# Windowed attention and a two-layer network in one kernel on Trainium2: in the list schedule of the later groups, the margin ahead of transposes and value products is doubled

## The chip, the cores and the metric

The kernel runs on one core of one Trainium2 chip. The metric is the device time of one execution in microseconds (us). The kernel before took 711.27 us, the median of three runs (710.24, 711.27 and 713.42).

## The reference

The inputs are q, k and v of 4 batches x 8 heads x 768 positions x 64, and two weights of 512 x 2048 and 2048 x 512, all float32. Each position attends to the first 8 positions and to the 96 behind and including itself, with a bias that falls with the distance; the heads are joined and go through a network with an ELU between its two layers.

```python
scores = scale * q @ k.T - slope[h] * dist          # slope[h] = 2 ** -(h + 1)
scores = where(is_global | is_local, scores, -1e9)  # is_global: column < 8; is_local: 0 <= row - column < 96
a = softmax(scores); attn = a @ v                   # per batch and head
x = attn, heads side by side: (4 * 768) x 512
h = x @ w_in
out = where(h > 0, h, exp(min(h, 0)) - 1) @ w_out   # (4 * 768) x 512
```

## The kernel before

**The work.** The 3072 positions are cut into 12 groups of 256 (two tiles of 128). For each group the kernel does attention for four pairs of heads (`pair`, which calls `head` once for each head of a pair) and then the network (`moe`) in 16 slices of 128 hidden columns. Products are split into a high and a low part, so a slice takes twelve matmuls 128x256 into a tile h (L606) and six matmuls 128x512 into the accumulators o (L628). Between them ACT and DVE make the ELU (L612 to L614), ACT rounds it to gh (L287 `copy`) and POOL takes the remainder gl (L295 `minus`).

**Attention of the later groups.** The first four groups take another path (`heads32`). From the fifth group on `head` does, for one head and each of its two tiles of positions: two matmuls for the scores s (L561); on DVE the table, the bias and the row's maximum (L478); on ACT the exponential and its sum (L480); once for both tiles the inverse on DVE (L487, L488); on DVE the scaling (L468); on PE one or two transposes of the probabilities pr into a tile t (L575); on ACT a rounding copy of t into pt (L287), on DVE the remainder into the other half of pt (L295); and on PE one or two value products of pt with vd into a tile pv (L587). When a head's two tiles are there, `pair` moves pv to x (ACT L287 once, DVE L459 twice), and after both heads of a pair x goes to xh (ACT) and xl (POOL), which the group's network reads. Each pair loads its q and v (rqv, L405) and its keys (rk, L406) by a DMA on SP's queue and splits them beforehand: qd (ACT L432), ks (ACT L287, then DVE L295 on 64 partitions), ql (DVE L437) and vd (POOL L289 and L295).

**Buffers.** The PSUM tiles have few slots: s two, h two, and t, pv, o0 and o1 one each. In the other memory pr has three slots, pt two, and rqv and rk one each.

**What sets the order.** Nothing is put in order by hand. `Plan.add` records each step with its cost, its engine, its reads and writes and a due time; `Plan.order` is a list scheduler that takes, over all five engines, the step that can start first and, among those that can start now, the one due first, and so fixes the order of each engine's queue. On the chip each engine then works through its queue in that order and waits at its head for what is not ready. The planner's durations are not the chip's. For a step on PE the planner lets it start only some time after its operands' planned end: a fixed 90 ns (`SEM`) and the step's `slack`. For the slot of a tile that the step is the first to write, only 0.3 of the slack is added:

```python
                    for of, t in op.ready.items():                                                          # L133
                        t = t + self.SEM + op.slack if of != e else t - self.LAT["PE"] if e == "PE" else t  # L135
                        at = max(at, t)                                                                     # L136
...
                        at = max(at, f + self.SEM + 0.3 * op.slack)                                         # L152
```

The steps with a slack are those of `head` on PE: the scores (L563), the transposes (L577) and the value products (L590). All have `SLACK` = 600 ns. The network's steps have none. While a margin runs, the planner gives PE other work that can start, mostly the network's matmuls of the group before.

## Time and profile before

| | |
|---|---|
| runs of the kernel before | 711.27 us median of 3 (710.24 to 713.42) |
| the profiled execution | 711.18 us, of which the span from first to last instruction 709.4 us |
| mean granted TensorE clock | 0.998 |
| busy: PE / PE weight loads / DVE / ACT / POOL | 98% / 87% / 73% / 71% / 35% of the span |
| transposes of the later groups (L575) | 240 matmuls, first at 212.3 us, last at 645.0 us |
| value products of the later groups (L587) | 240 matmuls, first at 215.9 us, last at 647.3 us |
| last matmul starts | 702.59 us |

In a row of the profile, PE is the matmul, PEld the loading of its stationary operand, DVE, ACT and POOL are the vector, scalar and general engines and SP is the one whose queue issues most DMAs. `out<-in` names the tiles that an instruction writes and reads. A timeline row gives the start (us), the time that it covers (us), engine, line, operation, tiles, how many instructions it stands for, and in brackets how long the engine sat idle just before and what ended that. Matmuls overlap, and their ends are modelled, so the distance from start to start tells more than the durations.

### The profile page before, as it was taken

To read this page: it belongs to the slowest core of one execution; us is meant where nothing else is said; L and a number is where in the kernel's file an instruction comes from. 1 tells how busy PE (TensorE), PEld (TensorE's weight loads), DVE (VectorE), ACT (ScalarE), POOL (GpSimd) and SP (SyncE) were. 2 spreads that over 40 slices of the span, in tenths; PEclk is the share of its full clock that TensorE was granted. 3 is DMA by queue.
4 is the path that set the end of the run, shared out by engine and by line. 5 is a ranking of instruction groups with operands and counts; after the bars stand their busy time and mean duration, and the time that the engine had idled before them with its cause. 6 is when DMAs were issued, how large, how long until landed. Compare 5 with 4: busy or idle time off the path is not lost.

```text
span 709.4 us, 13834 instructions
## 1 busy us (share of the span) xinstructions
PE 693.8 (98%) x4701; PEld 615.0 (87%) x4701; DVE 517.3 (73%) x1571; ACT 504.0 (71%) x1463; POOL 246.5 (35%) x274
## 2 busy tenths in 40 slices
PE   9989999999999999999999999999999999999996
PEld 6768888889898989999989999999989989999895
DVE  6999999996658958856766875884783884884322
ACT  6989887774657758867767876876776785875442
POOL 2430543440023443433453452542443354332000
PEclk9999999999999999999999999999999999999999
DMA  8443960000233212312312222230331321210000
GB/s 322 176 127 132 419 274 24 1 24 1 76 105 94 82 54 83 107 54 84 107 54 83 80 81 64 73 106 31 107 83 40 107 71 51 84 54 1 31 1 34
DMA packets 22254, 63.49 MB, mean 89 GB/s; under 512 B 2592, under 2 KB 4896, under 8 KB 22176
## 3 DMA queue, kind: packets, MB, share of 16 engines
q1 hardware_dynamic: 21888, 62.40, 26.3%
q8 instruction: 39, 0.64, 0.4%
q14 instruction: 39, 0.32, 0.1%
q10 hardware_dynamic: 288, 0.13, 0.1%
HBM read 56.23 MB, written 6.29 MB: 88 GB/s over the span
## 4 chain that ended last, share of the span: by engine, by line
PE 71%; DVE 16%; DMA 6%; ACT 4%; issue 2%; SPq 1%; DVEq 0%; ACTq 0%
PE h L606 29%; PE o L628 29%; PE pv L587 4%; PE s L561 4%; DMA bits<-in_w_out_dram 4%; PE t L575 3%; DVE g L372 2%; DVE g L374 2%; DVE e L614 2%; DVE w L295 1%; DVE gl L295 1%; DVE pr L478 1%; DVE ks L295 1%; DMA rqv<-in_qkv_dram 1%; DVE pr L468 1%
## 5 line engine op out<-in xcount | busy, mean ns | idle before, releaser
L606 PEld LDWEIGHTS h<-xh,w 128*128 128x128 f32 x1536 | 228.2, 189 | 26.5 <-issue 1.0
L606 PE MATMUL h<-xh,w 128*128 128x256 f32 x1536 | 245.7, 283 | 0.3 <-DVE e L614 0.3
L628 PE MATMUL o<-w,gh 128*128 128x512 f32 x768 | 243.7, 399 | 1.3 <-DVE w L295 0.4
L295 POOL TENSOR_TENSOR gl<-e,gh 128x256 fp32r<-128x256 f32 x133 | 101.8, 765 | 263.5 <-ACT gh L287 253.8
L628 PEld LDWEIGHTS o<-w,gh 128*128 128x128 f32 x768 | 126.2, 189 | 15.2 <-ACT gh L287 2.8
L614 DVE SCALAR_TENSOR_TENSOR e<-e,h 128x256 f32<-128x256 f32 x192 | 80.0, 417 | 73.0 <-ACT e L613 64.5
L628 PE MATMUL o<-w,gl 128*128 128x512 f32 x384 | 133.0, 400 | 0.0
L612 ACT ACTIVATE e<-h 128x256 f32<-128x256 f32 x192 | 73.3, 382 | 74.6 <-PE h L606 67.4
L606 PE MATMUL h<-xl,w 128*128 128x256 f32 x768 | 123.6, 283 | 0.0
L287 ACT CAST gh<-e 128x256 fp32r<-128x256 f32 x192 | 77.4, 403 | 54.1 <-DVE e L614 53.1
L606 PEld LDWEIGHTS h<-xl,w 128*128 128x128 f32 x768 | 104.2, 189 | 0.3 <-issue 0.2
L478 DVE CUSTOM_DVE_ANT_0 pr<-s,tab 128x256 f32<-128x256 f32 (+1 forms) x192 | 73.4, 395 | 42.5 <-PE s L561 37.5
L480 ACT ACTIVATE pr<-pr,nmax 128x256 f32<-128x256 f32 (+1 forms) x192 | 93.6, 488 | 13.4 <-DVE nmax L478 12.7
L613 ACT ACTIVATE e<-e 128x256 f32<-128x256 f32 x192 | 80.1, 418 | 4.2
L369 POOL TENSOR_SCALAR g<-g 128x512 f32<-128x512 f32 x25 | 54.3, 2180 | 69.9 <-ACT g L367 65.2
L459 DVE TENSOR_TENSOR x<-pv,x 64x256 f32<-64x256 f32 x128 | 53.7, 419 | 21.3 <-ACT x L287 18.7
L628 PEld LDWEIGHTS o<-w,gl 128*128 128x128 f32 x384 | 63.7, 189 | 2.2
L468 DVE TENSOR_SCALAR pr<-pr,st 128x256 f32<-128x256 f32 (+1 forms) x159 | 62.2, 421 | 1.2
L287 ACT CAST pt<-t 128x256 fp32r<-128x256 f32 (+1 forms) x128 | 45.5, 355 | 20.9 <-PE t L575 20.3
L295 DVE TENSOR_TENSOR pt<-t,pt 128x256 fp32r<-128x256 f32 (+1 forms) x128 | 51.5, 402 | 11.6 <-ACT pt L287 10.8
L575 PE MATMUL t<-ident,pr 128*128 128x128 f32 x240 | 47.4, 273 | 2.8 <-DVE pt L295 2.5
L587 PE MATMUL pv<-pt,vd 128*128 128x256 f32 x240 | 49.5, 289 | 0.1
(92 smaller groups left out, 880.7 us busy)
## 6 DMA issues: line engine op xcount, KB each, us to landing
rqv<-in_qkv_dram SPq DMA_DIRECT2D x32, 512.0 KB, 3.5
rk<-in_qkv_dram SPq DMA_DIRECT2D x32, 400.0 KB, 3.2
bits<-in_w_in_dram SPq DMA_DIRECT2D x16, 512.0 KB, 9.0
bits<-in_w_out_dram SPq DMA_DIRECT2D x16, 512.0 KB, 9.7
rqv<-in_qkv_dram SPq DMA_DIRECT2D x16, 384.0 KB, 3.6
out_dram<-ob SPq DMA_DIRECT2D x23, 256.0 KB, 2.0
rk<-in_qkv_dram SPq DMA_DIRECT2D x16, 200.0 KB, 4.8
out_dram<-ob ACTq DMA_DIRECT2D x1, 128.0 KB, 2.6
```

The costliest lines, as they stand in the source:

```text
L287: self.nc.scalar.copy(out, x)
L295: self.on(e).tensor_tensor(out, x, y, ALU.subtract)
L468: self.nc.vector.tensor_scalar(out, x, sc, None, ALU.mult)
L478: p.add((("DVE", 158 + 1.042 * n, False),), lambda e: nc.vector.tensor_tensor_reduce(pr.t[:, lo:], s.t[:, m, lo:], tab, -(2.0 ** -(h + 1)) ...
L480: p.add(act(n, extra=200), lambda e: nc.scalar.activation(pr.t[:, lo:], pr.t[:, lo:], AF.Exp, bias=nm, scale=-1.0, accum_out=st.t[:, 0, i: ...
L575: nc.tensor.transpose(tp.t[:, a], pr.t[:, a * P:(a + 1) * P], self.ident.t)
L587: nc.tensor.matmul(pv.t[:, i].rearrange("p s w -> p (s w)"), vd.t[:, 2 * i + a, j].rearrange("p s d -> p (s d)"), pt.t[:, a].rearrange("p ...
L606: nc.tensor.matmul(h.t, w1.t[:, s, cc * P:(cc + 1) * P], x.t[:, cc], start=n == 0 and cc == 0, stop=n == 2 and cc == self.NCC - 1)
L612: p.add(act(W, True), lambda e: nc.scalar.activation(ex.t, h.t, AF.Relu, scale=-1.0), [h], [ex], d - 8000)
L613: p.add(act(W), lambda e: nc.scalar.activation(ex.t, ex.t, AF.Exp, scale=-1.0), [ex], [ex], d - 8000)
L614: p.add(dve(W), lambda e: nc.vector.scalar_tensor_tensor(ex.t, ex.t, -1.0, h.t, ALU.add, ALU.max), [h, ex], [ex], d - 8000)
L628: nc.tensor.matmul(acc[i].t, g.t[:, i * P:(i + 1) * P], w2.t[:, s], start=fc == f0 and n == 0 and s == HI, stop=fc == f1 - 1 and n == 1)
```

## The change

The transposes and the value products get a margin of their own, `LATER` = 1200 ns; the scores keep 600 ns. Nothing is added or removed, and no duration, due time or slot changes. Since the planner's times move, so does the order of the steps on every engine from the fifth group's attention on.

```diff
@@ head
-            p.add((("PE", 75.0 * (2 - a0), False),), transposes, [pr], [tp], d - 2500, slack=slack)
+            p.add((("PE", 75.0 * (2 - a0), False),), transposes, [pr], [tp], d - 2500, slack=self.LATER)
...
-            p.add((("PE", 122.0 * (2 - a0), False),), values, [vd, pt], [pv], d, slack=slack)
+            p.add((("PE", 122.0 * (2 - a0), False),), values, [vd, pt], [pv], d, slack=self.LATER)
@@ class Kernel
-    SLACK = 600.0
+
+    SLACK, LATER = 600.0, 1200.0
```

The lines below `SLACK` move down by one (L786 becomes L787). Up to the first transpose of the fifth group PE's queue is the same row for row. Three places of the queues are shown, before and after the change. In the names the first number is that of the tile, the same in both kernels, and the second differs between them.

PE, in the seventh group's attention, around the two transposes t_1108 and t_1110 of one head; h_988 and h_992 are tiles of the network, pv and pt those of value products. Before:

```order
L575 MATMUL t_1108_5041<-ident_67,pr_1105_4956 128x128
L606 MATMUL h_988_5016<-xl_12_3944,w0_401_1735 128x256 x4
L628 MATMUL o_950_4535<-w1_392_1719,gl_983_4966 128x512
L628 MATMUL o_951_4578<-w1_392_1719,gl_983_4966 128x512
L628 MATMUL o_950_4535<-w1_398_1790,gh_986_5032 128x512 x2
L606 MATMUL h_992_5066<-xh_11_3928,w0_407_1863 128x256 x4
L575 MATMUL t_1110_5074<-ident_67,pr_1107_4964 128x128 x2
L587 MATMUL pv_1102_5078<-pt_1109_5047,vd_1099_4834 128x256
L628 MATMUL o_951_4578<-w1_398_1790,gh_986_5032 128x512 x2
```

And now, from the first four matmuls of h_992 on:

```order
L606 MATMUL h_992_5051<-xh_11_3956,w0_407_1863 128x256 x4
L628 MATMUL o_951_4573<-w1_398_1790,gh_986_5008 128x512 x2
L575 MATMUL t_1108_5064<-ident_67,pr_1105_4947 128x128
L606 MATMUL h_992_5051<-xh_11_3956,w0_407_1863 128x256 x4
L606 MATMUL h_992_5051<-xl_12_3962,w0_407_1863 128x256 x4
L587 MATMUL pv_1085_5029<-pt_1094_5036,vd_1072_4658 128x256 x2
L628 MATMUL o_950_4535<-w1_398_1790,gl_987_5019 128x512
L575 MATMUL t_1110_5091<-ident_67,pr_1107_4994 128x128 x2
```

t_1110 stood right behind the first four matmuls of h_992 and now stands behind two o, eight h and one o more of the network; t_1108 has moved by more than that, so fewer matmuls lie between the two. The value product of t_1108's pt, which stood right behind t_1110, now comes eight rows below it.

DVE, in the same place: the scaling of pr_1107 (L468), which t_1110 reads, the remainder of the next keys ks_1193 (L295, 64x800), and the remainder pt_1109 (L295), the last reader of t_1108. Before:

```order
L468 TENSOR_SCALAR pr_1107_4964<-pr_1107_4964,st_1103_4968 128x256
L295 TENSOR_TENSOR ks_1193_5022<-rk_1191_4902,ks_1193_5022 64x800
L459 TENSOR_TENSOR x_1074_4986<-pv_1085_5024,x_1074_4986 64x256
L478 ISA pr_1117_5055,nmax_71<-s_1116_5004,tab1_69 128x256
L478 ISA nmax_71 128x1
L295 TENSOR_TENSOR pt_1109_5047<-t_1108_5041,pt_1109_5047 128x128
```

And now:

```order
L468 TENSOR_SCALAR pr_1107_4994<-pr_1107_4994,st_1103_4956 128x256
L295 TENSOR_TENSOR ks_1193_5021<-rk_1191_4893,ks_1193_5021 64x800
L295 TENSOR_TENSOR pt_1094_5036<-t_1093_5016,pt_1094_5036 128x2x128
L437 SCALAR_TENSOR_TENSOR ql_1195_5058<-rqv_1190_4917,qd_1192_5014 128x256
L614 SCALAR_TENSOR_TENSOR e_989_5044<-e_989_5044,h_988_4997 128x256
L437 SCALAR_TENSOR_TENSOR ql_1195_5058<-rqv_1190_4917,qd_1192_5014 128x256
L478 ISA pr_1117_5072,nmax_71<-s_1116_5005,tab1_69 128x256
L478 ISA nmax_71 128x1
L295 TENSOR_TENSOR pt_1109_5074<-t_1108_5064,pt_1109_5074 128x128
```

Between ks and the remainder of t_1108 there were two steps, an addition to x and a softmax step; now there are five: the remainder of the tile before, two ql, an ELU step and the softmax step.

PE, at the end of the fifth group's attention, from its last value products on: up to the first matmul that reads the new group's xh_9. Before, the last value products stood here, and that first reader came six rows below the last row shown:

```order
L587 MATMUL pv_760_3562<-pt_769_3560,vd_747_3235 128x256 x2
L628 MATMUL o_599_2942<-w1_500_2115,gh_646_3543 128x512 x2
L606 MATMUL h_652_3576<-xh_7_2480,w0_509_2140 128x256 x4
L606 MATMUL h_652_3576<-xl_8_2482,w0_509_2140 128x256 x4
L628 MATMUL o_598_2907<-w1_500_2115,gl_647_3550 128x512
L628 MATMUL o_599_2942<-w1_500_2115,gl_647_3550 128x512
L628 MATMUL o_598_2907<-w1_506_2253,gh_650_3582 128x512 x2
L606 MATMUL h_656_3609<-xh_7_2480,w0_515_2263 128x256 x4
L628 MATMUL o_599_2942<-w1_506_2253,gh_650_3582 128x512 x2
L606 MATMUL h_656_3609<-xh_7_2480,w0_515_2263 128x256 x4
L606 MATMUL h_656_3609<-xl_8_2482,w0_515_2263 128x256 x4
```

And now, with that first reader in the last row:

```order
L587 MATMUL pv_760_3593<-pt_769_3590,vd_747_3237 128x256 x2
L606 MATMUL h_656_3604<-xh_7_2480,w0_515_2263 128x256 x4
L606 MATMUL h_656_3604<-xl_8_2482,w0_515_2263 128x256 x4
L628 MATMUL o_598_2907<-w1_506_2253,gl_651_3581 128x512
L628 MATMUL o_599_2939<-w1_506_2253,gl_651_3581 128x512
L561 MATMUL s_847_3632<-ks_841_3430,qd_840_3412 128x256
L561 MATMUL s_847_3632<-ks_841_3430,ql_843_3448 128x256
L628 MATMUL o_598_2907<-w1_512_2313,gh_654_3609 128x512 x2
L628 MATMUL o_599_2939<-w1_512_2313,gh_654_3609 128x512 x2
L606 MATMUL h_770_3647<-xh_9_3150,w0_78_408 128x256 x8
```

Eight matmuls of h, six of o and two of s are left between the last value products and the first reader of xh_9. That reader keeps its place in the network's work but for two matmuls of o that now come ahead of it; the value products have come closer to it.

## The prediction

> **What bounds the kernel now.** I read the page first, for which engine is full, then PE's timeline for its pace and for the places where it falls behind, and then DVE's and ACT's timelines at those places.
>
> From the page:
>
> ```profile
> PE 693.8 (98%) x4701; PEld 615.0 (87%) x4701; DVE 517.3 (73%) x1571; ACT 504.0 (71%) x1463; POOL 246.5 (35%) x274
> PEclk9999999999999999999999999999999999999999
> ```
>
> PE is busy from end to end at the full clock, so it sets the end. But these spans overlap, so I take PE's pace from the starts, in a stretch where it waits for nothing:
>
> ```profile
> 255.00 0.38 PE L575 MATMUL t<-ident,pr 128*128 128x128 f32 x2
> 255.14 0.72 PE L606 MATMUL h<-xl,w 128*128 128x256 f32 x4
> 255.70 0.40 PE L587 MATMUL pv<-pt,vd 128*128 128x256 f32 x2
> ...
> 257.33 0.39 PE L587 MATMUL pv<-pt,vd 128*128 128x256 f32 x2
> 257.56 0.62 PE L628 MATMUL o<-w,gh 128*128 128x512 f32 x2
> 258.02 0.63 PE L606 MATMUL h<-xh,w 128*128 128x256 f32 x4
> 258.50 0.63 PE L606 MATMUL h<-xl,w 128*128 128x256 f32 x4
> ```
>
> From start to start two value products take 0.23 us (257.56 - 257.33), two o 0.46 and four h 0.48. The four h behind a pair of transposes take 0.56, so that pair costs 0.14 and 0.08 behind it. I use 0.118 per h, s or value product, 0.231 per o and 0.22 per pair of transposes.
>
> Where a transpose or a value product starts later than this pace lets it, PE has waited. The places that carry the sum:
>
> ```profile
> 214.49 0.62 PE L628 MATMUL o<-w,gh 128*128 128x512 f32 x2
> 215.28 0.41 PE L575 MATMUL t<-ident,pr 128*128 128x128 f32 x2 [0.16 <-DVE st L487]
> ...
> 249.23 0.64 PE L606 MATMUL h<-xh,w 128*128 128x256 f32 x4
> 250.27 0.44 PE L575 MATMUL t<-ident,pr 128*128 128x128 f32 x2 [0.40 <-DVE pt L295]
> ...
> 357.68 0.63 PE L606 MATMUL h<-xh,w 128*128 128x256 f32 x4
> 359.04 0.41 PE L575 MATMUL t<-ident,pr 128*128 128x128 f32 x2 [0.74 <-DVE pt L295]
> 359.50 0.36 PE L587 MATMUL pv<-pt,vd 128*128 128x256 f32 x1
> ...
> 525.44 0.63 PE L606 MATMUL h<-xh,w 128*128 128x256 f32 x4
> 527.09 0.41 PE L575 MATMUL t<-ident,pr 128*128 128x128 f32 x2 [1.02 <-DVE pt L295]
> 527.55 0.36 PE L587 MATMUL pv<-pt,vd 128*128 128x256 f32 x1
> ...
> 583.56 0.63 PE L628 MATMUL o<-w,gh 128*128 128x512 f32 x2
> 584.54 0.41 PE L575 MATMUL t<-ident,pr 128*128 128x128 f32 x2 [0.35 <-DVE pt L295]
> ...
> 614.87 0.63 PE L606 MATMUL h<-xl,w 128*128 128x256 f32 x4
> 615.45 0.70 PE L587 MATMUL pv<-pt,vd 128*128 128x256 f32 x4
> ```
>
> At 249.23 four h take 0.47, but the transposes start 1.04 later: 0.57 of waiting, of which the bracket, with its modelled ends, shows 0.40. In the same way the others are 0.33 (215.28), 0.89 (359.04), 1.18 (527.09), 0.52 (584.54) and 0.11 (615.45), and each value product that follows its transposes at once comes 0.32 late (0.46 instead of 0.14, at 359.50 and 527.55). These are 4.2 us in eight places, the first and the last of the stretch among them. Thirteen smaller places (at most 0.20 each) bring the whole to 21 places and 5.75 us. About 3.95 us of it stand ahead of transposes, 0.9 ahead of value products that wait for pt, and 0.9 ahead of the first value products of a new pv tile. That is all that a larger margin can win, since the network's matmuls wait for nothing. Their idle time stands last in these rows of the groups by line, cut to the stretch from 212 to 660 us (the third row is used further down):
>
> ```profile
> L606 PE MATMUL h<-xh,w 128*128 128x256 f32 x1024 | 165.1, 283 | 0.0
> L628 PE MATMUL o<-w,gh 128*128 128x512 f32 x509 | 161.6, 398 | 0.0
> ...
> L432 ACT ACTIVATE qd<-rqv 128x256 fp32r<-128x256 f32 x61 | 25.4, 417 | 0.6 <-DMA rqv<-in_qkv_dram 0.3
> ```
>
> Nothing of PE's queue changes ahead of the fifth group's first transposes (215 us), and after 647 us there is no attention left. Both ends of the kernel stay as they are.
>
> **The change, part by part.** *Work:* none is added. PE's queue holds the same matmuls, 128 groups of transposes before and after, and none of them next to another, so the 0.08 behind each stays.
>
> *Positions.* Laid out at the pace above, the later orders differ as follows (medians over the 128 groups of transposes): a transposition comes 1.5 us later among the network's matmuls and a value product 1.9 us. The distance from a tile's scores to its transposes grows from 6.8 to 7.9 us (shortest: 4.1 to 4.7), from transposes to their value products from 2.3 to 2.9 (shortest: 1.85 to 2.55). From one group of transposes to the next it hardly grows (2.0 to 2.1; shortest 1.2 to 1.4): the slot of t gets 0.3 of the margin, 360 ns instead of 180.
>
> *The two large waits.* The bracket names DVE's pt, the last reader of the only t slot. What made it late is in DVE's rows of the first place:
>
> ```profile
> 356.05 1.72 DVE L295 TENSOR_TENSOR ks<-rk,ks 64x800 fp32r<-64x800 f32 x1 [0.27 <-ACT ks L287]
> 357.80 0.43 DVE L459 TENSOR_TENSOR x<-pv,x 64x256 f32<-64x256 f32 x1
> 358.26 0.42 DVE L478 CUSTOM_DVE_ANT_0 pr<-s,tab 128x256 f32<-128x256 f32 x1
> ...
> 358.61 0.29 DVE L295 TENSOR_TENSOR pt<-t,pt 128x128 fp32r<-128x128 f32 x1
> 358.93 0.43 DVE L459 TENSOR_TENSOR x<-pv,x 64x256 f32<-64x256 f32 x1
> 359.39 0.42 DVE L437 SCALAR_TENSOR_TENSOR ql<-rqv,qd 128x256 fp32r<-128x256 f32 x1
> 359.84 0.42 DVE L614 SCALAR_TENSOR_TENSOR e<-e,h 128x256 f32<-128x256 f32 x1
> 360.18 0.46 DVE L487 TENSOR_SCALAR st<-st 128x2 f32<-128x2 f32 x1
> ```
>
> The keys hold DVE until 357.77; then come two steps and pt, done at 358.90, and PE starts 0.14 later. Without the wait t_1110 would have started at 359.04 - 0.89 = 358.15. After the change it stands behind two o, eight h and one o more: 3 x 0.231 + 8 x 0.118 = 1.64, so at 359.8. But behind the keys DVE now has five steps ahead of that pt. From start to start an x takes 0.46, a ql 0.45, an ELU step 0.34 and L478 0.35; pt_1094, of the same size, lies between 0.34 and 0.45. With 0.40 for it that is 0.40 + 0.45 + 0.34 + 0.45 + 0.35 + 0.29 = 2.28, so pt is done at 360.05 and PE could start at 360.2. The wait shrinks from 0.89 to about 0.4, if the keys stay where they are: their load and their rounding on ACT carry no margin. The second place has the same order and keeps about 0.7. The value products behind both no longer follow at once, so 0.64 goes.
>
> *The rest, place by place.* The wait at 215.28 stays (its transposes have not moved, 0.33). Those at 250.27 and 584.54 belong to transposes that move by 0.9 and 1.4, more than they waited: 1.09 goes. So do the small ones ahead of transposes (0.5) and the 0.3 of pt's that are left. The 0.9 ahead of new pv tiles I leave: they wait for the additions to x that free the only pv slot, which has the small share of the margin too. Gone: 0.98 (the two large ones) + 0.64 + 1.09 + 0.5 + 0.3 = 3.5. Left: 2.3.
>
> *What is added.* A transposition that comes later keeps its pr and t longer, and pv is moved to x later. The planner has arranged all five queues around that, but with its own durations: the same lags of DVE will meet other places. No row prices this. Below, it is nothing; above, it is a whole new set of waits like the old, 5.75. I take 1.2, a fifth of that, because most margins have grown and the slots' have not shrunk. On SP some loads of rk and rqv change places with each other; both are issued ahead of need, and all 61 qd on ACT waited only 0.3 for their DMA, so I count nothing, and some tenths if one is late.
>
> *The sum.* 3.5 - 1.2 = 2.3 us. The profiled execution took 711.18 (span 709.4 and 1.8 around it), within 0.1 of the median of 711.27. So 711.2 - 2.3 = **708.9 us**, span about 707.1. The case's own range is 707.7 to 710.2, for added waits between 0 and 2.5.
>
> **The rivals.**
>
> *The slots bind (710.3).* Nearly all brackets ahead of transposes name pt, the reader of the single t slot. If those waits follow DVE, and DVE's steps behind the keys move along, then only the 0.9 ahead of value products that wait for pt goes: 711.2 - 0.9 = 710.3. For it: the same wait at 357.68 and at 525.44, one shape 168 us apart. Against it: the transposes move by 1.5 us, and the keys do not have to. The Trainium skill speaks for this rival (Perfetto Trace Analysis, Optimization Strategy): a gap that repeats on the engine that should be full can mean that there is no room for the next tile, and a margin adds no slot. The trace agrees so far that the gap repeats and that the slot's reader ends it.
>
> *The margin covers all (705.4 to 706.3).* If 600 ns more are taken off each wait, only 0.3 and 0.6 of the two largest are left: 711.2 - 4.9 = 706.3, and 705.4 if all 5.75 goes. For it: only two waits exceed 0.6. Against it: the slots' share of the margin grows by 180 ns alone.
>
> *The group's end comes too late (715.6).* The value products have come closer to the next group's first matmuls. Until xh stands there is a chain over ACT, DVE and ACT, here at the end of the fifth group and then inside the tenth:
>
> ```profile
> 257.78 0.36 ACT L287 COPY x<-pv 64x256 f32<-64x256 f32 x1
> ...
> 259.51 0.40 ACT L287 CAST xh<-x 128x256 fp32r<-128x256 f32 x1
> ```
>
> ```profile
> 522.65 0.52 PE L587 MATMUL pv<-pt,vd 128*128 128x256 f32 x3
> ```
>
> ```profile
> 527.43 0.41 ACT L287 CAST xh<-x 128x256 fp32r<-128x256 f32 x1
> ```
>
> From the first of the last value products (257.33, above) to the end of xh it took 259.91 - 257.33 = 2.6 us; inside a group, with the keys in DVE's way, 527.84 - 522.65 = 5.2. From those value products to the first reader of xh the order before left 5.6 us at the first group's end and 8.2 to 8.9 at the others. Now it leaves 10 x 0.118 + 6 x 0.231 + 2 x 0.118 = 2.8 at the first, 4.2 at two, and 5.1 to 6.3 at the other five. So it decides nothing at 2.6, and a chain of 5.2 would cost 2.4 + 2 x 1.0 = 4.4. In that case DVE lags as much as before elsewhere and I count no gain: 711.2 + 4.4 = 715.6. Against it: no keys stand in DVE's way at a group's end, and the chain took 2.6 or less there in all eight groups.
>
> **How the numbers follow.** About 0.5% (3.6 us) is what a measurement of this kernel can tell from no change. The forecast has 0.45, the slots 0.17, the margin that covers all 0.27, and the late group's end 0.11. The first two end within 0.5% (0.62), the third is faster (0.27), the fourth slower (0.11). The range goes from 705.4, where no wait is left, to 712.2: the slots' 710.3 and a third of the old waits (1.9) anew. It leaves out the fourth case.
>
> **What would show it.** In the profile after: 2 to 5 us of waiting, by starts, ahead of L576 and L588; the two large ones at 0.4 to 0.7; the value products behind them at distance; span 706 to 708.4; the same pace. It is wrong if the two places keep 0.9 and more, if waits of half a microsecond stand ahead of L607 at group ends, or if the network's matmuls (L607, L629), which wait for nothing now, wait for gh, gl or xh.

## The result and the profile after

| | before | after |
|---|---|---|
| median of 6 runs each, us | 711.67 (710.24 to 713.42) | 716.58 (715.06 to 717.15) |
| ratio, 95% interval | | 1.0056 (1.0040 to 1.0072) |
| profiled execution, us | 711.18 | 715.68 |
| its span, us | 709.4 | 713.9 |
| last matmul starts at, us | 702.59 | 707.33 |

The changed kernel is slower by 0.56%, 4.9 us between the medians and 4.5 between the two spans. The forecast was 708.9, with a range up to 712.2. In the page of after, PE does the same work at the same clock:

```profile
PE 694.3 (97%) x4701; PEld 611.4 (86%) x4701; DVE 518.6 (73%) x1571; ACT 503.9 (71%) x1463; POOL 243.2 (34%) x274
PEclk9999999999999999999999999999999999999999
```

PE is busy for 0.5 us more in a span that is 4.5 longer, so the time is waiting. The groups of after by line, cut to 212 to 667 us, show in front of what it stands (idle time and its releaser last):

```profile
L606 PE MATMUL h<-xh,w 128*128 128x256 f32 x1030 | 166.3, 284 | 0.0
...
L587 PE MATMUL pv<-pt,vd 128*128 128x256 f32 x240 | 49.5, 286 | 1.1 <-ACT e L612 1.1
L575 PE MATMUL t<-ident,pr 128*128 128x128 f32 x240 | 47.6, 274 | 3.7 <-DVE pt L295 3.5
```

The network's matmuls, L606 above, still show no idle time. (The prediction's L576, L588, L607 and L629 are L575, L587, L606 and L628 in this profile.)

I count waits as the prediction does: by starts, beyond 0.118 us per h, s or value product, 0.231 per o and 0.22 per pair of transposes, at all places of more than 0.05 us after 205 us. Here are the sums for every run, in us, each from the run's profiled execution. "Network" is the matmuls of h and o; those of the scores have no column (0.2 to 0.3 in before and after, up to 3.1 in values_scaling_on_act). The last column is the ratio to the kernel before on the same chip. The runs stand on several chips, on which the kernel before took 711.67 to 712.57, so times of different runs are best compared by their ratios.

| run | transposes | value products | flag | network | median us | ratio (95%) |
|---|---|---|---|---|---|---|
| before | 4.07 | 1.80 | 0.16 | 0.54 | 711.67 | |
| after | 6.41 | 1.96 | 1.51 | 0.71 | 716.58 | 1.0056 (1.0040 to 1.0072) |
| two_halves_before | 2.63 | 1.97 | 0.16 | 0.49 | 711.40 | 0.9989 (0.9976 to 1.0002) |
| two_halves_after | 4.37 | 2.62 | 1.50 | 0.70 | 716.08 | 1.0057 (1.0042 to 1.0072) |
| slot_margin_full | 0.11 | 0.45 | 1.48 | 6.45 | 714.62 | 1.0036 (1.0020 to 1.0051) |
| flag_later | 6.44 | 1.95 | 0.09 | 0.70 | 714.22 | 1.0025 (1.0011 to 1.0039) |
| transposes_only | 2.74 | 7.45 | 1.28 | 1.63 | 718.76 | 1.0108 (1.0093 to 1.0122) |
| values_only | 4.11 | 0.00 | 0.16 | 0.63 | 711.77 | 0.9996 (0.9985 to 1.0006) |
| slot_600 | 2.33 | 4.02 | 1.28 | 0.57 | 714.56 | 1.0036 (1.0023 to 1.0049) |
| gl_an_eighth | 2.04 | 0.47 | 1.51 | 0.55 | 709.31 | 0.9957 (0.9943 to 0.9972) |
| gl_an_eighth_before | 2.64 | 2.06 | 0.09 | 0.53 | 709.81 | 0.9974 (0.9962 to 0.9986) |
| eighth_and_flag | 0.94 | 0.31 | 0.09 | 0.62 | 708.17 | 0.9947 (0.9931 to 0.9963) |
| margin_900 | 3.57 | 2.92 | 0.09 | 0.43 | 711.85 | 0.9997 (0.9983 to 1.0011) |
| scaling_two_inputs | 8.55 | 2.52 | 1.50 | 0.95 | 724.37 | 1.0166 (1.0143 to 1.0188) |
| values_and_two_inputs | 11.77 | 0.00 | 0.16 | 0.43 | 723.05 | 1.0162 (1.0139 to 1.0185) |
| values_scaling_on_act | 4.10 | 1.49 | 1.56 | 0.58 | 717.51 | 1.0076 (1.0055 to 1.0098) |
| gl_on_vector_before | 3.40 | 1.62 | 0.93 | 0.95 | 717.69 | 1.0093 (1.0066 to 1.0120) |
| gl_on_vector_values | 6.11 | 0.15 | 0.09 | 0.60 | 720.11 | 1.0125 (1.0102 to 1.0148) |

**The old waits are gone.** This is PE of after at the transposes that waited 0.89 us at 359.04 before. They start 0.23 us behind one o, which is the pace, and nothing is lost:

```profile
360.78 0.39 PE L628 MATMUL o<-w,gl 128*128 128x512 f32 x1
361.01 0.38 PE L575 MATMUL t<-ident,pr 128*128 128x128 f32 x2
361.14 0.47 PE L628 MATMUL o<-w,gl 128*128 128x512 f32 x1
```

Taken tile by tile, 3.5 us of waiting ahead of transposes and 1.7 ahead of value products have gone.

Why this wait is gone is seen on DVE and POOL. The remainder of the keys took 1.72 us before (356.05, in the prediction). This is POOL of before at that time, and then DVE of after with the same step and the pt behind it:

```profile
355.51 1.41 POOL L295 TENSOR_TENSOR vd<-rqv,vd 128x512 fp32r<-128x512 f32 x1
356.88 1.49 POOL L295 TENSOR_TENSOR gl<-e,gh 128x256 fp32r<-128x256 f32 x1
```

```profile
357.56 0.99 DVE L295 TENSOR_TENSOR ks<-rk,ks 64x800 fp32r<-64x800 f32 x1
...
360.31 0.29 DVE L295 TENSOR_TENSOR pt<-t,pt 128x128 fp32r<-128x128 f32 x1
```

Before, the keys' step lay beside two GpSimd operations. In after GpSimd is idle from 357.18 to 360.19, and the step takes 0.99, which is also what it takes elsewhere with GpSimd idle. At the second place it went from 1.42 to 0.99. Transposes did not get more room there: counted at PE's pace, their distance to the transposes before them fell from 1.87 to 1.41 us at both places.

**New waits have come.** Ahead of transposes 6.0 us are new, ahead of value products 2.0. The largest part stands at one place of the heads' order that comes five times: from the last tile of one head to the first tile of the next. It is PE of after at the third of these:

```profile
447.27 0.41 PE L575 MATMUL t<-ident,pr 128*128 128x128 f32 x2
447.44 0.72 PE L606 MATMUL h<-xh,w 128*128 128x256 f32 x4
447.99 0.63 PE L606 MATMUL h<-xl,w 128*128 128x256 f32 x4
448.46 0.40 PE L587 MATMUL pv<-pt,vd 128*128 128x256 f32 x2
448.70 0.63 PE L628 MATMUL o<-w,gl 128*128 128x512 f32 x2
449.83 0.41 PE L575 MATMUL t<-ident,pr 128*128 128x128 f32 x2 [0.50 <-DVE pt L295]
```

Two o take 0.46, so the transposes could have started at 449.16 and wait 0.67. DVE of after and POOL of after at the same place show why the pt that frees the slot is late:

```profile
447.79 0.40 DVE L459 TENSOR_TENSOR x<-pv,x 64x256 f32<-64x256 f32 x1
448.11 0.90 DVE L468 TENSOR_SCALAR pr<-pr,st 128x256 f32<-128x256 f32 x1
448.93 0.41 DVE L478 CUSTOM_DVE_ANT_0 pr<-s,tab 128x256 f32<-128x256 f32 x1
...
449.27 0.41 DVE L295 TENSOR_TENSOR pt<-t,pt 128x256 fp32r<-128x256 f32 x1
449.61 0.33 DVE L468 TENSOR_SCALAR pr<-pr,st 128x256 f32<-128x256 f32 x1
```

```profile
448.03 0.83 POOL L295 TENSOR_TENSOR gl<-e,gh 128x256 fp32r<-128x256 f32 x1 [1.05 <-ACT gh L287]
```

The scaling L468 takes 0.90 us at 448.11 and 0.33 at 449.61. The first one meets a subtraction on GpSimd and ends 0.15 behind its end (449.01 against 448.86). Before the change, this slow scaling stood at the same place of the program, but no transposes were near. Here are DVE, POOL and PE of before:

```profile
445.99 0.42 DVE L295 TENSOR_TENSOR pt<-t,pt 128x256 fp32r<-128x256 f32 x1
446.32 0.41 DVE L459 TENSOR_TENSOR x<-pv,x 64x256 f32<-64x256 f32 x1
446.65 1.08 DVE L468 TENSOR_SCALAR pr<-pr,st 128x256 f32<-128x256 f32 x2
```

```profile
446.59 0.73 POOL L295 TENSOR_TENSOR gl<-e,gh 128x256 fp32r<-128x256 f32 x1 [1.08 <-ACT gh L287]
```

```profile
444.14 0.38 PE L575 MATMUL t<-ident,pr 128*128 128x128 f32 x2
...
447.65 0.38 PE L575 MATMUL t<-ident,pr 128*128 128x128 f32 x2
```

The pt was done ahead of the slow scaling, and 3.5 us lay between the two groups of transposes instead of 2.56. By the order at PE's pace the distance at this place has fallen from 3.04 to 1.64 us, in all five heads. A second place, also in five heads, fell from 2.10 to 1.87. The first class now waits 0.61 to 0.69 each (3.3 us), the second 0.20 to 0.49 (1.8 us); neither waited before.

**The flag.** One wait is of a kind that the prediction does not have. The program puts nine small DVE steps and a matmul for the flag into the order 60 operations behind the last transposes. PE of after, then DVE of after, and then PE of before:

```profile
661.62 0.62 PE L606 MATMUL h<-xh,w 128*128 128x256 f32 x4
663.59 0.19 PE L787 MATMUL flagsum<-one,flag 128*1 128x1 f32 x2 [1.35 <-DVE flag L783]
```

```profile
661.88 0.42 DVE L614 SCALAR_TENSOR_TENSOR e<-e,h 128x256 f32<-128x256 f32 x1 [2.37 <-ACT e L613]
662.22 0.35 DVE L775 TENSOR_REDUCE flag<-nmax 128x1 f32<-128x192 f32 x1
...
663.28 0.16 DVE L783 TENSOR_REDUCE flag<-flag 128x1 f32<-128x6 f32 x1
```

```profile
657.30 0.63 PE L628 MATMUL o<-w,gl 128*128 128x512 f32 x2
657.93 0.19 PE L786 MATMUL flagsum<-one,flag 128*1 128x1 f32 x2
```

DVE of before, at the first and the last of the nine steps:

```profile
656.05 0.35 DVE L774 TENSOR_REDUCE flag<-nmax 128x1 f32<-128x192 f32 x1
...
657.62 0.16 DVE L782 TENSOR_REDUCE flag<-flag 128x1 f32<-128x6 f32 x1
```

Counted in operations the steps stand where they stood. Before, PE came to the flag's matmul at 657.8, when DVE was through. Now PE has done the four h ahead of it by 662.09, before DVE begins, and waits 1.5 us instead of 0.16.

The sum: 2.3 (transposes) + 0.2 (value products) + 1.35 (flag) = 3.9 of the 4.5 us between the spans; with the network's and the places under 0.05 us it is 4.6, and the last matmul starts 4.7 later.

### The profile page after: what moved, and what is told of

Its sections match the earlier page's. It is cut to its first block, busy times and chain, and to the rows that moved or that the text cites. A ratio compares the mean times of both kernels' runs of the same rounds, so it can differ in the third digit from the quotient of the medians.

```text
span 713.9 us, 13833 instructions
## 1 busy us (share of the span) xinstructions
PE 694.3 (97%) x4701; PEld 611.4 (86%) x4701; DVE 518.6 (73%) x1571; ACT 503.9 (71%) x1463; POOL 243.2 (34%) x274
## 4 chain that ended last, share of the span: by engine, by line
PE 66%; DVE 21%; ACT 5%; DMA 5%; issue 2%; POOL 0%; SPq 0%; DVEq 0%; ACTq 0%
PE h L606 28%; PE o L628 27%; PE pv L587 3%; PE s L561 3%; PE t L575 3%; DMA bits<-in_w_out_dram 2%; DVE e L614 2%; DVE pr L478 2%; DVE g L372 2%; DVE g L374 2%; DVE pr L468 2%; DMA rqv<-in_qkv_dram 1%; DVE w L295 1%; DVE x L459 1%; DVE pt L295 1%
## 5 line engine op out<-in xcount | busy, mean ns | idle before, releaser
L606 PEld LDWEIGHTS h<-xh,w 128*128 128x128 f32 x1536 | 226.2, 189 | 24.1 <-issue 1.0
L606 PE MATMUL h<-xh,w 128*128 128x256 f32 x1536 | 245.9, 283 | 0.3 <-DVE e L614 0.3
L628 PE MATMUL o<-w,gh 128*128 128x512 f32 x768 | 243.9, 400 | 1.1 <-ACT gh L287 0.5
L295 POOL TENSOR_TENSOR gl<-e,gh 128x256 fp32r<-128x256 f32 x133 | 103.8, 781 | 266.2 <-ACT gh L287 238.7
L628 PEld LDWEIGHTS o<-w,gh 128*128 128x128 f32 x768 | 125.7, 189 | 14.1 <-ACT gh L287 2.8
L628 PE MATMUL o<-w,gl 128*128 128x512 f32 x384 | 134.0, 404 | 0.0
L606 PE MATMUL h<-xl,w 128*128 128x256 f32 x768 | 122.8, 282 | 0.0
L606 PEld LDWEIGHTS h<-xl,w 128*128 128x128 f32 x768 | 104.3, 189 | 0.3 <-issue 0.2
L369 POOL TENSOR_SCALAR g<-g 128x512 f32<-128x512 f32 x25 | 55.8, 2241 | 68.4 <-ACT g L367 63.7
L628 PEld LDWEIGHTS o<-w,gl 128*128 128x128 f32 x384 | 63.4, 189 | 2.3
L468 DVE TENSOR_SCALAR pr<-pr,st 128x256 f32<-128x256 f32 (+1 forms) x159 | 63.9, 431 | 1.3
L295 DVE TENSOR_TENSOR pt<-t,pt 128x256 fp32r<-128x256 f32 (+1 forms) x128 | 51.5, 402 | 9.7 <-ACT pt L287 7.8
L575 PE MATMUL t<-ident,pr 128*128 128x128 f32 x240 | 47.6, 274 | 3.7 <-DVE pt L295 3.5
L587 PE MATMUL pv<-pt,vd 128*128 128x256 f32 x240 | 49.5, 286 | 1.1 <-ACT e L612 1.1
```

Of the source, the lines that this page charges most:

```text
L295: self.on(e).tensor_tensor(out, x, y, ALU.subtract)
L468: self.nc.vector.tensor_scalar(out, x, sc, None, ALU.mult)
L575: nc.tensor.transpose(tp.t[:, a], pr.t[:, a * P:(a + 1) * P], self.ident.t)
L587: nc.tensor.matmul(pv.t[:, i].rearrange("p s w -> p (s w)"), vd.t[:, 2 * i + a, j].rearrange("p s d -> p (s d)"), pt.t[:, a].rearrange("p ...
L606: nc.tensor.matmul(h.t, w1.t[:, s, cc * P:(cc + 1) * P], x.t[:, cc], start=n == 0 and cc == 0, stop=n == 2 and cc == self.NCC - 1)
L628: nc.tensor.matmul(acc[i].t, g.t[:, i * P:(i + 1) * P], w2.t[:, s], start=fc == f0 and n == 0 and s == HI, stop=fc == f1 - 1 and n == 1)
```

## The experiments

The first theory was: the change costs what the shorter spacing of transposes over their single slot costs, and the flag. Its rivals: the transposes' lateness itself costs; or the group's end. Later a second question came up: whether the spacing is short by itself, or because VectorE's scaling is slow beside GpSimd.

**A slot in two halves.** In both orders, the groups of transposes take the two halves of t's slot in turn:

```diff
+            tp.make = self.half          # one [P, 2, 2, P] tile, halves in turn
```

> The changed kernel with its instruction order unchanged, but the one slot of t split into two halves that the transposes of the later groups use in turn, so that a group of transposes waits for the last reader of the tile before the previous one. Slot theory (the new waits ahead of transposes are for DVE's remainder pt, the last reader of the only t slot): the waits ahead of the transposes, 6.8 us in the changed kernel, fall below 2.5, and the time to 711.5 to 713. Operand theory (the transposes wait for their own pr, which DVE scales late): at most 1 us goes, 715.5 to 717.

> The kernel before with its order unchanged and the t slot split into two halves used in turn. Slot theory: the waits ahead of transposes fall from 4.0 us to about 1, time 708.5 to 709.5 where the kernel before takes 711.7. Operand theory: 711 to 712.

Measured: 716.08 and 711.40 us; against the kernel before on the same chip neither ratio moved (1.0057 after 1.0056, and 0.9989). The first class still waits 0.52 to 0.62. The edit did not do what it says: in neither run does a group of transposes start before the pt of the tile before it has ended, at the earliest 0.05 us behind it, as without the edit. So the half that was free was not used; that the two halves are one tile to the framework is the likely reason, not shown. That the waits ahead of transposes are 2.0 and 1.4 us less all the same stays open; the times show no gain. So these two runs neither support nor refute the slot, and a second slot for t was not tried.

**The full margin for the slot, at 1200.**

```diff
-                        at = max(at, f + self.SEM + 0.3 * op.slack)
+                        at = max(at, f + self.SEM + (1.0 if v.cls == "t" else 0.3) * op.slack)
```

> The changed kernel, but the planner adds the whole margin (1200 ns) and not 0.3 of it behind the release of t's slot; the shortest distance from one group of transposes to the next grows from 1.4 to 2.3 us. Slot theory: waits ahead of transposes below 2 us, time 711 to 713. Re-roll theory (any new order meets DVE's lags somewhere, whatever the distances): 714 to 718.

Measured: 714.62 us. Waits ahead of transposes are gone (0.11), but the network's matmuls wait 6.45. PE of this run, at the end of the fifth group's attention:

```profile
267.89 0.60 PE L606 MATMUL h<-xh,w 128*128 128x256 f32 x3
270.17 0.85 PE L606 MATMUL h<-xh,w 128*128 128x256 f32 x5 [1.68 <-ACT xh L287]
```

This wait is the late group's end of the prediction. The change alone did not reach it; a still later attention does. The other four network waits of half a microsecond or more in this run (0.5 to 0.7, at 440, 465, 608 and 634 us) are for the ELU step or gh. So the slot theory had the transposes' waits right (below 2), and the other theory the time.

**The flag later.**

```diff
-                if i == last + 60:
+                if i == last + 72:
```

> The changed kernel, with the check of the row maxima (nine small steps on DVE and a matmul that sums them) recorded 72 and not 60 steps behind the last transposes. All theories: the 1.5 us that PE waits for that matmul falls to 0.3 or less, nothing else moves, so 1.0 to 1.3 us less than the changed kernel: 715.2 to 715.6. If that wait is not on the path that sets the end: 716.6.

Measured: 714.22 us, and the flag's wait is 0.09 instead of 1.51. The ratio goes from 1.0056 to 1.0025, about 2.2 us, where 1.0 to 1.3 were expected; the two intervals leave room for that. The flag is shown to be a part of the loss, and not all of it.

**One half of the change at a time.** Either line alone gets `slack=self.LATER`:

```diff
 # transposes_only: the line of the transposes;  values_only: the line of the value products
-            p.add(..., slack=slack)
+            p.add(..., slack=self.LATER)
```

> The long margin for the transposes alone; the value products keep 600. In the order the five places of the first class (second tile of one head, then first tile of the next) stand 1.87 us behind the transposes before them (3.04 before the change, 1.64 with the whole of it), those of the second class 2.10 (2.10 before, 1.87 with the whole of it). Theory (the cost of the change is the spacing of the transposes, since all share one slot): the first class waits 0.3 to 0.45 us each, the second not at all, waits ahead of transposes 3.0 to 4.5 us in all, the flag about 0.2 (its matmul stands behind an output product), so 711.0 to 713.5 us. Rival (the late transposes themselves cost, whatever their spacing): as after, 715 to 717 us.

> The long margin for the value products alone; the transposes keep 600. In the order the first class stands 3.27 us behind the transposes before it, the second 1.88, and the flag's matmul stands where it stood before the change. Theory (spacing): the first class waits for nothing, the second 0.2 to 0.5 us each, the waits of the value products fall from 1.8 to under 1.0, the flag stays near 0.2; 711 to 713.5 us. Rival (the longer distance of the value products is what costs): 714 us or more, with the first class waiting 0.6 as after.

Measured: 718.76 and 711.77 us. For the value products alone the theory's forecast held in the main: no wait in the first class, and the value products' own waits are all gone (1.80 to 0.00). But the second class, 1.88 us apart, waits for nothing either, where 0.2 to 0.5 each were expected: the spacing alone does not set the wait. The groups of this run by line, 212 to 660 us:

```profile
L587 PE MATMUL pv<-pt,vd 128*128 128x256 f32 x240 | 49.9, 286 | 0.0
L575 PE MATMUL t<-ident,pr 128*128 128x128 f32 x240 | 47.9, 275 | 1.5 <-DVE pt L295 1.1 <-DVE st L487 0.2
```

The transposes wait as much as before (4.11), mostly at other places, and the time is the same. For the transposes alone both theories missed. Spaced 1.87 us apart, the first class waits for nothing and the transposes only 2.74 in all; the value products wait 7.45, in 25 places, and most of that right behind an addition to x. PE and DVE of this run at one of them:

```profile
305.48 0.40 PE L628 MATMUL o<-w,gl 128*128 128x512 f32 x1
306.52 0.47 PE L587 MATMUL pv<-pt,vd 128*128 128x256 f32 x2 [0.64 <-DVE x L459]
```

```profile
304.65 0.43 DVE L459 TENSOR_TENSOR x<-pv,x 64x256 f32<-64x256 f32 x1
305.11 0.61 DVE L487 TENSOR_SCALAR st<-st 128x2 f32<-128x2 f32 x1
...
305.95 0.43 DVE L459 TENSOR_TENSOR x<-pv,x 64x256 f32<-64x256 f32 x1
```

The inverse (L487, and L488 behind it), which the next transposes need, has moved in between the two additions to x that free the only pv slot, and the value products did not move with it. Its first step takes 0.61 here, beside gl on GpSimd (304.96 to 305.69); with GpSimd idle it takes 0.17 at most in after. The longer margin of the value products is what covers this in the whole change. So there are two single slots here, t's and pv's, and each half of the change alone moves the wait from one to the other.

**The slot's margin at 600.** The kernel before, with the line of the full slot margin above.

> The kernel before, with the margin of the shared slot of the transposes raised from 180 to the full 600 ns; no operand has the longer margin. In the order no two transposes stand less than 1.86 us apart (before: 39 under 1.7), the first class 3.05, the second 2.80. Theory (spacing of the shared slot): waits ahead of transposes fall from 4.1 to under 2, no matmul of the network waits more than 0.3 at a group's end; 708.5 to 710.5 us, below the kernel before. Rival (any longer margin ahead of transposes gives its time back at the group's end, as the run with 1200 did): 711 to 714 us with half a us or more ahead of network matmuls.

Measured: 714.56 us. The transposes wait 2.33, less than before, but the first value products of a pv tile wait 4.02 and the flag 1.28. The theory missed, for the same reason as with the transposes alone.

**Without the slow scalings.** After's order, with GpSimd's gl of the later groups an eighth as wide:

```diff
-                        for g, s in ((gh, HI), (gh, LO)) if n == 0 else ((gl, HI),):
+                        for g, s in ((gh, HI), (gh, LO)) if n == 0 else ((gl if X else gh, HI),):
...
-lambda e: self.minus(e, gl.t, ex.t, gh.t)
+lambda e: self.minus(e, *(v.t[:, :32] if e == "POOL" and not X else v.t for v in (gl, ex, gh)))
```

> After's order, instruction by instruction; the low halves gl of the later groups are made by GpSimd in 32 columns of 256, and the matmuls that read them read gh in their place, so the low part of these products is left out. Theory (the chain behind the first class is long because VectorE's scaling of the probabilities takes 0.90 us beside GpSimd's subtraction and 0.33 without it): no scaling above 0.6 us beside gl, the five waits of 0.61 to 0.69 fall below 0.15, those of the second class stay within 0.15 of their 0.20 to 0.49, waits ahead of transposes fall from 6.4 to 3 or less, the flag's 1.4 stays: 712 to 714 us. Rival (a spacing of 1.64 us is too short whatever VectorE does beside it): the five waits keep 0.4 or more and the time stays at 715 to 717.

Measured: 709.31 us, below before (0.9957) and 1.0% below after by the two ratios, about 7 us. That is below both forecasts: the value products' waits fell too, from 1.96 to 0.47, which the theory had not counted. DVE, POOL and PE of this run at the place shown above:

```profile
444.15 0.34 DVE L468 TENSOR_SCALAR pr<-pr,st 128x256 f32<-128x256 f32 x1
444.41 0.41 DVE L478 CUSTOM_DVE_ANT_0 pr<-s,tab 128x256 f32<-128x256 f32 x1
...
444.75 0.41 DVE L295 TENSOR_TENSOR pt<-t,pt 128x256 fp32r<-128x256 f32 x1
```

```profile
443.97 0.26 POOL L295 TENSOR_TENSOR gl<-e,gh 128x32 fp32r<-128x32 f32 x1 [0.28 <-ACT gh L287]
```

```profile
445.09 0.62 PE L628 MATMUL o<-w,gh 128*128 128x512 f32 x2
445.55 0.38 PE L575 MATMUL t<-ident,pr 128*128 128x128 f32 x2
```

The scaling takes 0.34 instead of 0.90, pt starts 0.60 us behind the scaling's start instead of 1.16, and the transposes follow the o at once. All five places of the first class have lost their wait. Of all 128 scalings, 8 still take over 0.55 us (25 in after), most of them beside GpSimd's work on vd. The second class keeps 1.5 us of its 1.8 (0.02 to 0.55 each; all were expected within 0.15 of the old wait). Slow scalings do not make it: in after no step of VectorE takes over 0.43 in the 2.6 us ahead of any of its five places.

The control is the same edit in the order of before.

> The order of the kernel before, with GpSimd's gl of the later groups in 32 columns of 256 and the matmuls that read it reading gh (the low part of these products is left out). It is the control for the same edit in after's order, which took 709.3 us, 7.3 below after. Theory (the change loses where it brings the transposes into VectorE's slow scalings, so without these most of its loss is gone): before gains only 2 to 3.5 us, to 708.5 to 710 us, and after's order, without the flag's 1.4, is level with it or below. Rival (the slow scalings cost both orders the same, and the change's loss is elsewhere): before gains about 7 us, to 704 to 706.

Measured: 709.81 us. The edit takes 1.0% off after's order (1.0056 to 0.9957) and 0.26% off before's, so the two end level, although after's order still waits 1.51 for the flag. So what gl does to VectorE's steps explains the change's loss apart from the flag: without it, the change no longer costs anything. The edit frees not the scalings alone but also VectorE's other steps beside gl, such as ql, the keys' remainder and the inverse; that the scaling is the one that counts is shown by the rows at the first class.

**Both causes away.** After's order with an eighth of gl and the flag at 72.

> After's order with gl of the later groups in 32 columns of 256 (matmuls read gh in its place, the low part is left out) and the flag's step 72 operations behind the last transposes in place of 60. If the change's loss is the sum of slow scalings and the flag, both are gone here, and what is left is what the forecast counted: 709.3 less the flag's 1.4, that is 707.4 to 708.5 us, below the run before-with-gl-an-eighth (709.8) by 1.3 to 2.4. Rival (the flag's wait is work that only moves to the end, or the two overlap): 709 us or more, level with it.

Measured: 708.17 us, with 0.94 ahead of transposes, 0.31 ahead of value products and 0.09 for the flag. The ratio is 0.9947 against 0.9974 for before's order with the same gl (the intervals just touch). So about the gain that was forecast, 0.3%, is there underneath when the new waits are not, at the edge of what these runs can tell.

**Is it the margin's length?** The change with 900 in place of 1200.

```diff
-    SLACK, LATER = 600.0, 1200.0
+    SLACK, LATER = 600.0, 900.0
```

> The change with 900 in place of 1200. In the order the first class stands 3.51 us behind the transposes before it, the second 1.86; the flag's matmul stands behind a network's first products as in after. Theory (spacing where the scaling is slow, place by place): the first class waits for nothing, the second 0.2 to 0.5 us each, value products under 1.5 us in all, the flag 1.2 to 1.5; 712 to 714.5 us. Rival (the longer the margin, the later the transposes and the more they cost, evenly): half of the change's loss, 714 us with the first class waiting 0.3 each.

Measured: 711.85 us, as before (0.9997), not half the loss. The first class, 3.51 us apart, waits for nothing; the second waits 0.08 to 0.14, less than the theory had it, and the flag 0.09, where the theory had 1.2 to 1.5 from the same neighbours. The value products wait 2.92, where it had under 1.5. This order also meets GpSimd less often: 11 of its 128 scalings take over 0.55 us, against 19 before and 25 in after. Here the sign hangs on the places, not on the length.

**Which operations share something with GpSimd?** After's order, and then the long margin for value products alone, with the scaling written with two inputs:

```diff
-            e, pr.t[:, lo:], pr.t[:, lo:], st.t[:, 2, i:i + 1])            # tensor_scalar
+            pr.t[:, lo:], pr.t[:, lo:], st.t[:, 2, i:i + 1], pr.t[:, lo:], ALU.mult, ALU.min)   # scalar_tensor_tensor
```

> After's order; the scaling of the probabilities on VectorE as a scalar_tensor_tensor, min(p / sum, p), with the same result (the sum is at least 1), in place of a tensor_scalar; GpSimd's gl in full. In the rows of after, two-input operations of VectorE take 0.42 us (x from pv and x, e from e and h, pt from t and pt: no stretched one among them), and all these have one input that the matmuls wrote; of the operations with one input, the scaling alone is stretched (0.35 to 0.90 and more beside gl). Theory A (only the one-input form shares something with GpSimd): no scaling takes over 0.5 us, the five waits of 0.61 to 0.69 fall below 0.25, 710.5 to 713 us. Theory B (any VectorE operation whose inputs are all in SBUF shares it): scalings of 0.6 us or more remain beside gl, 15 or more of them, the five waits keep 0.5 or more, 715 to 717.5 us. Theory B is what the Trainium skill says (SBUF — State Buffer, on engine ports: operations with both inputs in SBUF contend with GpSimd's reads).

> The long margin for the value products alone, which took 711.8 us against 711.9 before (value products wait for nothing there, transposes 4.1 us), with the scaling as in the run of two inputs. Theory A: the waits of the transposes fall to 2 to 3 us, 709 to 711 us, below the kernel before by 0.1 to 0.4%. Theory B: 711 to 713 us, no better than before.

Measured: 724.37 and 723.05 us. Theory B held in kind and was too mild in size. The rows of after could have told it beforehand, for "no stretched one among them" leaves out two steps with both inputs in SBUF: ql takes 0.43 us at most with GpSimd idle and up to 0.95 beside it, the keys' remainder (64x800) 0.99 and up to 1.48. Nor is the scaling the only step with one input that is stretched: the first step of the inverse (L487) takes 0.17 with GpSimd idle and up to 1.30 beside it. The scaling's group in the later part (205 to 700 us; busy time, then the mean of one in ns), of after, of gl_an_eighth and of this run:

```profile
L468 DVE TENSOR_SCALAR pr<-pr,st 128x256 f32<-128x256 f32 x112 | 47.2, 448 | 1.1
```

```profile
L468 DVE TENSOR_SCALAR pr<-pr,st 128x256 f32<-128x256 f32 x112 | 38.1, 367 | 1.1
```

```profile
L494 DVE SCALAR_TENSOR_TENSOR pr<-pr,st 128x256 f32<-128x256 f32 x112 | 59.4, 556 | 1.1
```

Of 128 scalings, 27 still take over 0.55 us (25 in after), and the others are longer than a tensor_scalar (median 0.48 instead of 0.35). 12 us more of VectorE ahead of pt cost 7.8 us more in the end (1.0166 against 1.0056).

**Versions with all work done that might beat both.** Half of the scalings on ScalarE (the planner may choose, with values_only's margins), and all gl subtractions on VectorE:

```diff
-            self.norm(pr, lo, st, i, d - 3000, False)
+            self.norm(pr, lo, st, i, d - 3000, True)
...
-            p.add((dve(W, port=True) if X or last else ()) + pool(W), ...
+            p.add(dve(W, port=True), ...
```

> The long margin for the value products alone, and the planner may put the scaling of the later groups' probabilities on ScalarE or VectorE (it puts 80 of 159 on ScalarE). A version that may beat both kernels: the result is the same. Theory (half of the scalings leave the engine that shares with GpSimd, and ScalarE, busy 71%, has room): waits ahead of transposes under 3 us, value products under 0.5, the flag under 0.5; 708.5 to 711 us. Rival (ScalarE, 0.4 us or more for each, comes late with the copies of transposes and with the network's exponentials): transposes and network matmuls wait 6 us or more, 713 to 716 us.

> The kernel before with all gl subtractions made on VectorE (0.42 us each by the rows of its two-input operations), none on GpSimd; the planner makes its order anew, and all work is done. Theory (the slow scalings beside GpSimd's gl set the waits ahead of transposes): scalings over 0.55 us fall from 19 to under 8, and with VectorE's busy share up from 73% to about 80% the kernel gains what the eighth gave it, 709 to 711 us. Rival (VectorE, with 54 us more, comes late with the copies): waits ahead of transposes rise to 6 us or more, 713 to 716 us.

> The long margin for the value products alone, all gl on VectorE, the flag's step at 72; all work is done. Transposes of the first class 3.27 us apart, of the second 2.33. Theory: value products wait under 0.5 us, transposes under 3, the flag under 0.2: 708.5 to 710.5 us, below both kernels. Rival (VectorE late): 712 to 716 us.

Measured: 717.51, 717.69 and 720.11 us. All three miss. With half of the scalings on ScalarE, only 4 of VectorE's take over 0.55 us, and still the transposes keep 4.10, the scores wait 2.1 for VectorE's part of the keys, and the flag waits 1.56: fewer slow scalings alone do not make a good order. With gl on VectorE, 14 scalings over 0.55 us are left in gl_on_vector_before, where under 8 were expected, now beside vd and xl. And the edit did more than it should: it took the choice of engine from the first groups too, and there VectorE comes late. Two long waits of PE stand there, 1.6 us for w at 55 us and 2.1 for the ELU step at 93 us; in before the longest wait of the network's matmuls is 0.4. The first transposes of the later groups start at 218.7 us (before: 212.4), and from there to the last matmul it takes 490.7 us (before: 490.2). The 6 us are lost ahead of the part in question, and within it nothing is won. No version with all the work done beat the kernel before; level with it are values_only, margin_900 and two_halves_before.

## Why the prediction was wrong, point by point

**What bounds the kernel: right.** PE did the same work at the same clock before and after, and most of the time went where PE waits ahead of transposes and value products.

**What goes: right in kind, too small.** 3.5 us were forecast; 5.2 went. The two large waits were to shrink to 0.4 and 0.7, and are gone. That part is luck: the forecast took the keys' step as it stood, 1.72 and 1.42 us, and did not see that GpSimd beside it had stretched it. In after the pt ends 0.41 us ahead of the transposes at the first place and 0.36 at the second; with the old lengths of the keys' step, and 0.15 from the end of pt to PE's start, waits of about 0.5 and 0.2 would have stayed, an estimate from these rows. The 0.33 at 215.28 that was to stay is gone as well. The waits of first value products for a free pv slot, which the forecast left in place, went too: values_only shows that the margin of the value products takes all of these.

**What is added: the step that failed.** "I take 1.2, a fifth of that, because most margins have grown and the slots' have not shrunk." The new waits are 8.0 us, and 1.35 for the flag. The first reason was true by its own count, but it is about the operands, and the new waits ahead of transposes are for pt, the slot's reader. The second was false. The slots' margins did shrink, at two classes of places among others: "From one group of transposes to the next it hardly grows (2.0 to 2.1; shortest 1.2 to 1.4)" was read from the median and the shortest of 128. It hid five places that fell from 3.04 to 1.64 and five from 2.10 to 1.87. A median says nothing of the places where a margin is used up, and the bound that stood there, 5.75, was no bound either: new waits can be more than the old ones.

**What makes 1.64 too short.** With a short gl the same 1.64 us is enough (gl_an_eighth). What uses it up is VectorE in between: a scaling that takes 0.90 us beside GpSimd's subtraction. The prediction read DVE's rows where PE waited before, and took durations from there as fixed. The rows of the places to which transposes move were in the trace of before: 1.08 us for two scalings at 446.65, beside the subtraction at 446.59. The Trainium skill (SBUF — State Buffer, Who interferes with whom) states a mechanism that fits: VectorE and GpSimd share a pair of ports as an exclusive lock, and tensor_scalar is among the operations that can take it. The traces agree: in after, 25 of 128 scalings take over 0.55 us, and every one ends 0.08 to 0.15 us behind the end of an operation on GpSimd; the 63 that meet none take 0.36 at most. They agree as well with what that section says of operations with both inputs in SBUF (scaling_two_inputs, and ql in after). That VectorE's steps slowed by gl make the loss apart from the flag is shown by gl_an_eighth and its control; that the lock is the mechanism is argued from these ends, not shown apart.

**The flag: not in the prediction.** "Both ends of the kernel stay as they are" was about its work. A step that is put at a fixed count of operations behind another moves against the rest of the order. flag_later shows that it costs 1.4 us of waiting.

**The rivals.** That the slots bind had half of the mechanism, one slot whose reader sets the time, but still counted a gain of 0.9 and no loss. The rule of the Trainium skill that was named there (Perfetto Trace Analysis, Optimization Strategy) points the right way: the waits do sit at single slots, those of t and of pv. But room for the next tile in the order alone does not settle it: with a full margin for t's slot the time moved to the network or to pv's slot (slot_margin_full, slot_600). The late group's end, the rival on the slower side, gave nearly the right time (715.6) by luck: no network matmul waits at a group's end in after. It comes only in slot_margin_full.

**What would show it.** The test that the prediction named for itself, 2 to 5 us ahead of transposes and value products, came out at 8.4. Its list of what would make it wrong (the two places, the group's ends, the network's matmuls) held none of what did.

## What to carry to other kernels

When a planner's margin moves instructions, list for each place how far the user of a single slot stands from the one before it, before and after, not the median over all. Then read the other engines' rows at the places that lose: a distance of 1.41 us cost nothing where VectorE's steps ran undisturbed, and 1.64 cost 0.6 where one of them met GpSimd. A longer margin is not a gain in one direction: it draws the places anew, and here 900 was level with 600 where 1200 lost 0.56%. Steps that are put into the order at a fixed count (a flag, a final sum) have to be followed one by one.

## What the runs showed of the hardware

A scaling of 128x256 on VectorE takes 0.33 to 0.36 us alone and up to 1.28 in after when a GpSimd operation is under way; it then ends with that operation, 0.08 to 0.15 us later. VectorE operations that read a matmul's result (the additions to x, the ELU step, the softmax step) take 0.43 at most beside GpSimd, as without it. Steps with both inputs in SBUF are stretched as the scaling is: ql took 0.43 at most with GpSimd idle and up to 1.00 beside it in before, the keys' remainder of 64x800 0.99 and up to 1.72. Writing the scaling with two SBUF inputs did not avoid the collision and took 0.48 at the median, so the change of form alone cost 7.8 us here.
